# Pooled attention and a tanhshrink FFN on one core: the row of score maxima turned by VectorE instead of TensorE and DRAM

## The chip, the cores and the metric

The kernel runs on one core of a Trainium2 chip. The metric is device time in microseconds (us) of one execution, as the median of several runs. The engines are TensorE (PE for matmuls, PEld for its weight loads), VectorE (DVE), ScalarE (ACT), GpSimd (POOL) and SyncE (SP), which here issues the DMAs.

## The reference

```python
def _attn_ref(q, k, v):                     # q, k, v: (8, 8, 1152, 64) float32
    B, H, S, D = q.shape
    q_pool = q.reshape(B, H, S // 2, 2, D).mean(axis=3)
    scores = (1.0 / np.sqrt(D)) * np.matmul(q_pool, k.transpose(0, 1, 3, 2))
    scores = scores - np.max(scores, axis=-1, keepdims=True)
    attn = np.exp(scores)
    attn = attn / (np.sum(attn, axis=-1, keepdims=True) + 1e-09)
    return np.matmul(attn, v)

def _moe_ref(x, w_in, w_out):               # x (4608, 512), w_in (512, 2048), w_out (2048, 512)
    h = x @ w_in
    g = h - np.tanh(h)
    return g @ w_out
...
    x = attn_out.transpose(0, 2, 1, 3).reshape(B * S, H * D)
    return _moe_ref(x=x, **moe_kwargs)
```

## The kernel before

The work is two stages in a row on one core: attention for 64 heads, then the FFN over 4608 tokens. All products run in the 32-bit format fp32r, and each operand is split into a high part and a rest (`hi`, `lo`), so that a product is the sum of three matmuls. Blocks of FFN weights are split in the same way during the attention, through a PSUM buffer (`w_block`).

Attention takes two heads at a time, a pair, 32 pairs in all. Heads lie on partitions 0 to 63 and 64 to 127. A pair has 36 units (`U`); the first 18 are the scores, the exponentials and the product with v for the first 288 queries, the other 18 the same for the other 288. At every second unit `scores` makes one group: four products of two heads each (`hi·hi`, `hi·lo`, `lo·hi` and `ones_k·mb`, 128 keys by 288 queries) into one PSUM buffer `ps`, and ACT takes the exponential of it into `p_f`. The fourth product subtracts the row of maxima: `mb` holds, on a partition of each head, minus the maximum of each query's scores, and `ones_k` has ones there. At a half's end `pv` multiplies the `p_f` with v, and behind the second half `z_sums` adds up the denominators.

The maxima are made beforehand, one or two pairs ahead. `max_part` multiplies 128 queries with 384 keys in one `hi` part, and DVE reduces the result from PSUM into `mx`; 15 such chunks make a pair. Eight of them run between the groups of the second half, seven between those of the first. `max_rows` then reduces `mx` to `nm`, 128 queries by 10 columns, and turns it into rows: PE transposes it with an identity at the start of the next half (`turn`), ACT copies the high part (`hi`), DVE takes the rest (`lo`), one DMA writes both to DRAM (`m_dram`), and four DMAs bring them back as two rows for each head of `mb`.

```python
        units = dict(load=-80, query_sums=-62, hi=-55, lo=-36, load_v=-30)
        row, steps = -19, (5, 11)
        ...
        if pi == 0:
            row, steps = -43, (3, 4)
```

These numbers are units before a pair's first group; `row` says when `max_rows` runs, `steps` how many units later the store and the loads of the row are put on SP's queue. Each engine runs its instructions in the order in which the units issue them (`InOrder`); all of it passes through the helper's line 37, so the profile gives that line and the names of tiles tell the instructions apart. SP's queue is in order as well: a DMA that waits holds back all behind it, and each waits for the DMA eight places ahead of it in the queue, whose semaphore it shares.

`ps` is a pool of four buffers of two PSUM banks each, for the groups, the chunks, p·v, the transposes and the weight blocks. A request is given the buffer whose last reader stands earliest in the program's order.

Of the kernel before, what the change touches and what calls it, by code (L numbers as in the profile page):

```python
# [8 lines left out]
F32 = mybir.dt.float32  # L9
F32R = mybir.dt.float32r  # L10
I32 = mybir.dt.int32
AF = mybir.ActivationFunctionType
ALU = mybir.AluOpType
AX = mybir.AxisListType
# [29 lines left out]
def kernel(  # L44
# [17 lines left out]
    nc = tc.nc  # L62
    P = 128
    B, NP, _, _, SQ = q.shape
# [10 lines left out]
    dram = ctx.enter_context(tc.tile_pool(name="scratch", bufs=1, space=DRAM))  # L75

    ident = const.tile([P, P], F32, name="ident")
# [9 lines left out]
    x_dram = dram.tile([NP, P, NTOK], F32, name="x_dram")  # L87
    z_dram = dram.tile([B, NP, 2, SQ], F32, name="z_dram")
    r_dram = dram.tile([B, NP, 2, SQ], F32, name="r_dram")
    m_dram = dram.tile([2, 10, 2, P], F32, name="m_dram")  # L90
    wi_dram = dram.tile([NF, P, 2, NP, P], F32, name="wi_dram")
    wo_dram = dram.tile([NF, P, 2, DM], F32, name="wo_dram")

# [41 lines left out]
    t, n = chunks.pop()  # L135
# [4 lines left out]
    with ExitStack() as actx:  # L140

        sm = actx.enter_context(tc.tile_pool(name="sm", bufs=2))
        op = actx.enter_context(tc.tile_pool(name="op", bufs=1))
# [7 lines left out]
        pe, act, dve, pool, sp = (InOrder(tc, e) for e in (nc.tensor, nc.scalar, nc.vector, nc.gpsimd, nc.sync))  # L151

        HQ = SQ // 2
        CH = S // 3
# [5 lines left out]


        mb = [op.tile([P, SQ], F32R, name=f"mb{i}") for i in range(2)]
        ones_k = op.tile([P, P], F32R, name="ones_k")
        for x in (*mb, ones_k):
            nc.gpsimd.memset(x.bitcast(F32), 0.0)
        for h in range(2):
            nc.gpsimd.memset(ones_k[64 * h:64 * h + 2].bitcast(F32), 1.0)


        at, first, early = {}, {}, {}  # L170

        def banks(dtype=F32):
            return ps_a.tile([P, 2, 512], dtype, name="ps")
# [3 lines left out]
        def add(u, f, *args, at=at):  # L177
            at.setdefault(u, []).append(lambda: f(*args))
# [22 lines left out]
        def query_sums(pi, eng):  # L201

            w = pairs[pi]
            eng.tensor_tensor(w.kq[:, 0:SQ], w.q_n[:, 0], w.q_n[:, 1], op=ALU.add)
            w.mx = sm.tile([P, 5, 2, 3], F32, name="mx")
            w.hi = hl.tile([P, KQ], F32R, name="hi")
            w.lo = hl.tile([P, KQ], F32R, name="lo")

# [8 lines left out]
        def max_part(u, pi, t, c):  # L217


            w = pairs[pi]  # L220
            ps = banks()
            q0 = min(t * P, SQ - P)
            mv = slice(SQ + c * CH, SQ + (c + 1) * CH)
            for h in range(2):
                r = slice(64 * h, 64 * h + 64)
                pe.matmul(ps[:, h, 0:CH], w.hi[r, q0:q0 + P], w.hi[r, mv], start=True, stop=True)
            add(u + 1, lambda: dve.tensor_reduce(w.mx[:, t, :, c], ps[:, :, 0:CH], axis=AX.X, op=ALU.max), at=first)

        def max_rows(u, pi, steps):

            w = pairs[pi]
            nm = sm.tile([P, 10], F32, name="nm")
            dve.tensor_reduce(nm, w.mx.rearrange("p t h c -> p (t h) c"), axis=AX.X, op=ALU.max, negate=True)
            mt = sm.tile([10, 2, P], F32R, name="mt")
            md = m_dram[w.i]

            def turn():
                w.ps_t = banks()[0:10, 0, 0:P]
                pe.transpose(w.ps_t, nm, ident)

            def hi():
                act.activation(mt[:, 0], w.ps_t, AF.Copy)

            def lo():
                dve.tensor_tensor(mt[:, 1], w.ps_t, mt[:, 0].bitcast(F32), op=ALU.subtract)

            def there():
                sp.dma_start(md, mt.bitcast(F32))

            def back():  # L250
                by_head = md.rearrange("(t h) s n -> h s t n", h=2)
                for h in range(2):
                    rows = w.mb[64 * h:64 * h + 2].bitcast(F32)
                    sp.dma_start(rows[:, 0:4 * P].rearrange("s (t n) -> s t n", n=P), by_head[h, :, 0:4])
                    sp.dma_start(rows[:, 4 * P:], by_head[h, :, 4, 5 * P - SQ:])
            add(u + 1, turn, at=first)
            add(u + 2, hi, at=first)
            add(u + 3, lo, at=first)
            add(u + steps[0], there)
            add(u + steps[1], back)  # L260

        def scores(w, half, kt, p):

# [138 lines left out]
        for i, blk in enumerate(blocks):  # L402
            u = U * (i - 2) + 5 if i else 23
# [17 lines left out]
        for i, t in enumerate((wi, wi, wi, wo, wi, wo)):  # L421
            f = len(t)
# [4 lines left out]
        for pi in range(n_pair):  # L427
            u = pi * U
            units = dict(load=-80, query_sums=-62, hi=-55, lo=-36, load_v=-30)
            row, steps = -19, (5, 11)  # L430

            spots = [x for half, us in ((-54, (2, 4, 8, 10, 12, 14, 16)), (-36, (2, 4, 8, 10, 14, 16)))
                     for x in [(early, half)] + [(at, half + i) for i in us]]
            if pi == 0:
                units.update(load=-70, query_sums=-62, hi=-60, lo=-41, load_v=-40)
                spots = [(at, -60 + i) for i in range(15)]
                row, steps = -43, (3, 4)
            if pi == 1:
                units.update(load=-104)
            add(u + units["load"], load, pi)  # L440
            add(u + units["query_sums"], query_sums, pi, dve if pi < 1 else pool)
            for c in range(0, KQ, SQ):
                add(u + units["hi"], hi_part, pi, c, c + SQ)
            add(u + units["lo"], lo_part, pi)
            for i, (when, x) in enumerate(spots):
                add(u + x, max_part, u + x, pi, i // 3, i % 3, at=when)
            add(u + units["load_v"], load_v, pi)
            add(u + row, max_rows, u + row, pi, steps)

        def run(u, at=at):  # L450

# [8 lines left out]
        for u in range(end + 60):  # L460
            run(u, first)
            run(u, early)
            n, r = divmod(u, G)
# [21 lines left out]
    pe, pool, sp = (InOrder(tc, e) for e in (nc.tensor, nc.gpsimd, nc.sync))  # L485
# [81 lines left out]
    for ci, (t0, n) in enumerate(chunks):  # L567
        x_h, x_l, _ = xs
        po = []
        for fc in range(NF):  # L570
# [11 lines left out]
            g = hidden(x_h, x_l, n, fc)  # L582
# [44 lines left out]
```

## Time and profile before

| what | value |
|---|---|
| median of 3 runs | 1634.48 us (1634.25 to 1634.59) |
| profiled execution | 1634.2 us, span 1632.4 us |
| busy share of the span | PE 99%, PEld 76%, DVE 75%, ACT 63%, POOL 53% |
| DMA queue of SP | 72512 packets, 145.80 MB, 27.3% of 16 engines |
| attention | from the start to about 835 us |
| FFN | from there to the end |

A row of the timeline gives start and length in us, engine, line, operation, output and inputs, shape, how many in a row, and in brackets how long the engine sat idle before it and what ended that. A row of a group gives busy time in us, mean length in ns, and idle time ahead of it. "issue" as a releaser means that the profile shows nothing that the engine waited for. Matmuls overlap, so the length of one is not the time until the next; that is read from the starts.

### The profile page before, as it was taken

The numbers are of one execution on the slowest core, as the hardware profiler recorded it, in microseconds if no ns is written. First come the engines' busy times: TensorE is split into PE (matmuls) and PEld (weight loads), VectorE is DVE, ScalarE is ACT, GpSimd is POOL, SyncE is SP. The second block draws the span as 40 slices with busy tenths as digits, with TensorE's granted clock in tenths as the row PEclk, the third lists the DMA queues.
The fourth block names the chain that finished last, engine by engine and source line by source line (L and its number), as shares of the span: only waits on it lengthen the run. The fifth ranks groups of instructions, "written<-read, shape, count | busy, mean of one in ns | idle before, by whom it ended". The sixth has DMA issues, their size and how long they took to land.

```text
span 1632.4 us, 32106 instructions
## 1 busy us (share of the span) xinstructions
PE 1611.2 (99%) x12576; PEld 1246.3 (76%) x12576; DVE 1226.8 (75%) x1725; ACT 1023.4 (63%) x1865; POOL 873.3 (53%) x694
## 2 busy tenths in 40 slices
PE   6999999999999999999999999999999999999999
PEld 3777777777777777777778888888888888888898
DVE  7877778787777777777648776777777777777786
ACT  2656665666556656665566666666665766666786
POOL 2776767667667676676754243434343342423332
PEclk9999999999999999999999999999999999999999
DMA  3343443443434434344546111101010111000000
GB/s 142 121 139 117 140 134 108 127 130 133 127 108 142 134 114 126 123 140 146 157 177 229 39 39 35 31 26 53 26 53 26 39 40 39 27 33 20 33 21 27
DMA packets 72664, 147.86 MB, mean 91 GB/s; under 512 B 11136, under 2 KB 36672, under 8 KB 72512
## 3 DMA queue, kind: packets, MB, share of 16 engines
q1 hardware_dynamic: 72512, 145.80, 27.3%
q8 instruction: 99, 1.62, 0.4%
q14 instruction: 53, 0.43, 0.1%
HBM read 109.49 MB, written 36.27 MB: 89 GB/s over the span
## 4 chain that ended last, share of the span: by engine, by line
PE 97%; DVE 2%; ACT 0%; DMA 0%; issue 0%; ACTq 0%
PE ps L37 49%; PE ps_h L37 24%; PE ps_o L37 24%; DVE mx L37 1%; DMA q_n<-in_q_dram 0%; ACT hi L37 0%; ACT p_f L37 0%; DVE lo L37 0%; DVE kq L37 0%; DVE w L37 0%; DVE ps L37 0%; ACT x L562 0%; ACT z_s L37 0%; ACT mt L37 0%; DVE nm L37 0%
## 5 line engine op out<-in xcount | busy, mean ns | idle before, releaser
L37 DVE TENSOR_REDUCE mx<-ps 128x2 f32<-128x768 f32 x480 | 434.8, 951 | 139.0 <-PE ps L37 138.9
L37 POOL TENSOR_TENSOR g_lo<-g_s,g_hi 128x512 fp32r<-128x512 f32 (+1 forms) x160 | 190.7, 1192 | 483.1 <-ACT g_hi L530 445.0
L37 ACT ACTIVATE p_f<-ps 128x576 f32<-128x576 f32 x576 | 362.7, 650 | 83.5 <-PE ps L37 67.4
L37 POOL TENSOR_TENSOR z<-p_f 128x576 f32<-128x576 f32 x192 | 275.2, 1433 | 236.7 <-ACT p_f L37 236.7
L37 PE MATMUL ps<-hi 64*128 64x288 f32 (+1 forms) x2112 | 318.0, 355 | 13.4 <-ACT hi L37 8.3
L37 PE MATMUL ps_h<-x,wi 128*128 128x512 f32 (+1 forms) x1440 | 318.3, 370 | 0.0
L37 PE MATMUL ps_o<-wo,g_hi 128*128 128x512 f32 x1008 | 311.7, 391 | 0.0
L37 PE MATMUL ps<-p_f,v 128*64 128x288 f32 x2304 | 293.5, 409 | 0.1
L37 PEld LDWEIGHTS ps_h<-x,wi 128*128 128x128 f32 x1440 | 253.3, 188 | 50.3
L37 PEld LDWEIGHTS ps<-hi 64*128 64x128 f32 x2112 | 195.8, 188 | 79.8 <-DVE mx L37 22.9
L37 PEld LDWEIGHTS ps<-p_f,v 128*64 128x64 f32 x2304 | 159.8, 137 | 113.7 <-ACT p_f L37 12.2
L519 ACT ACTIVATE g_u<-ps_h 128x512 f32<-128x512 f32 (+1 forms) x160 | 88.8, 555 | 236.3 <-PE ps_h L37 236.3
L524 DVE SCALAR_TENSOR_TENSOR ps_w<-g_u,ps_h 128x512 f32<-128x512 f32 (+1 forms) x160 | 103.2, 645 | 157.6 <-ACT g_t L520 157.0
L37 PEld LDWEIGHTS ps_o<-wo,g_hi 128*128 128x128 f32 x1008 | 187.7, 188 | 39.0
L37 PE MATMUL ps_o<-wo,g_lo 128*128 128x512 f32 x504 | 196.4, 390 | 0.0
L37 POOL TENSOR_TENSOR z<-z,p_f 128x576 f32<-128x576 f32 x128 | 183.1, 1431 | 10.0
L37 ACT ACTIVATE o_s<-ps 128x288 f32<-128x288 f32 x64 | 26.3, 411 | 231.8 <-PE ps L37 231.8
L37 PE MATMUL ps<-lo,hi 64*128 64x288 f32 x1152 | 171.2, 294 | 0.0
L37 PE MATMUL ps<-hi,lo 64*128 64x288 f32 x1152 | 171.1, 293 | 0.0
L37 PE MATMUL ps<-mb,ones_k 64*128 64x288 f32 x1152 | 170.6, 292 | 0.0
L529 DVE COPY_PREDICATED g_s<-g_m,g_t 128x512 f32<-128x512 int32 (+1 forms) x160 | 115.1, 719 | 16.7 <-DVE g_s L528 0.5
L527 DVE SCALAR_TENSOR_TENSOR ps_w<-g_s,ps_w 128x512 f32<-128x512 f32 (+1 forms) x160 | 102.9, 643 | 16.6 <-ACT g_m L523 0.5
(70 smaller groups left out, 2248.3 us busy)
## 6 DMA issues: line engine op xcount, KB each, us to landing
q_n<-in_q_dram SPq DMA_DIRECT2D x32, 576.0 KB
kq<-in_k_dram SPq DMA_DIRECT2D x32, 576.0 KB
v<-in_v_dram SPq DMA_DIRECT2D x32, 576.0 KB
x_dram<-o_s SPq DMA_DIRECT2D x32, 288.0 KB
out_dram<-o_s SPq DMA_DIRECT2D x34, 256.0 KB
w_raw<-in_moe_w_in_dram SPq DMA_DIRECT2D x16, 512.0 KB
wi_dram<-w_hl SPq DMA_DIRECT2D x16, 512.0 KB
w_raw<-in_moe_w_out_dram SPq DMA_DIRECT2D x16, 512.0 KB
```

Of the source, the lines that this page charges most:

```text
L37: ins = self.tc.keep_in_program_order(f(*args, **kwargs))
L519: nc.scalar.activation(u, h, AF.Square)
L524: nc.vector.scalar_tensor_tensor(w, u, -P0, h, op0=ALU.add, op1=ALU.mult)
L527: nc.vector.scalar_tensor_tensor(w, s2, P2, w, op0=ALU.add, op1=ALU.mult)
L529: last = nc.vector.copy_predicated(s1, m.bitcast(I32), th).ins
```

## The change

The turn of the maxima leaves PE, ACT and DRAM. `nm` becomes a fixed tile of 128 x 32 whose columns 10 to 31 stay zero; DVE transposes it in blocks of 32 by 32 right behind the reduction, so that in `tr` the row of column c lies on partitions c, c + 32, c + 64 and c + 96, 32 queries on each. Ten DMAs, one for each head and group of 128 queries, put these pieces straight into one row of `mb` for each head. The row goes in one part instead of a high part and a rest, so `ones_k` has one row of ones for each head. The order inside `mx` is heads first. The DMAs stand at `row` + 3, and for pair 0 at `row` + 1.

```diff
-    m_dram = dram.tile([2, 10, 2, P], F32, name="m_dram")
...
+        nms = [op.tile([P, 32], F32R, name=f"nm{i}") for i in range(2)]
...
-        for x in (*mb, ones_k):
+        for x in (*nms, *mb, ones_k):
...
-            nc.gpsimd.memset(ones_k[64 * h:64 * h + 2].bitcast(F32), 1.0)
+            nc.gpsimd.memset(ones_k[64 * h:64 * h + 1].bitcast(F32), 1.0)
...
-            w.mx = sm.tile([P, 5, 2, 3], F32, name="mx")
+            w.mx = sm.tile([P, 2, 5, 3], F32, name="mx")
...
-        def max_rows(u, pi, steps):
+        def max_rows(u, pi, step):
...
-            nm = sm.tile([P, 10], F32, name="nm")
-            dve.tensor_reduce(nm, w.mx.rearrange("p t h c -> p (t h) c"), axis=AX.X, op=ALU.max, negate=True)
-            mt = sm.tile([10, 2, P], F32R, name="mt")
-            md = m_dram[w.i]
-            def turn():
-                w.ps_t = banks()[0:10, 0, 0:P]
-                pe.transpose(w.ps_t, nm, ident)
-            def hi():
-                act.activation(mt[:, 0], w.ps_t, AF.Copy)
-            def lo():
-                dve.tensor_tensor(mt[:, 1], w.ps_t, mt[:, 0].bitcast(F32), op=ALU.subtract)
-            def there():
-                sp.dma_start(md, mt.bitcast(F32))
+            nm, tr = nms[w.i], sm.tile([P, 32], F32, name="tr")
+            dve.tensor_reduce(nm[:, 0:10], w.mx.rearrange("p h t c -> p (h t) c"), axis=AX.X, op=ALU.max, negate=True)
+            dve.transpose(tr, nm.bitcast(F32))
             def back():
-                by_head = md.rearrange("(t h) s n -> h s t n", h=2)
-                for h in range(2):
-                    rows = w.mb[64 * h:64 * h + 2].bitcast(F32)
-                    sp.dma_start(rows[:, 0:4 * P].rearrange("s (t n) -> s t n", n=P), by_head[h, :, 0:4])
-                    sp.dma_start(rows[:, 4 * P:], by_head[h, :, 4, 5 * P - SQ:])
-            add(u + 1, turn, at=first)
-            add(u + 2, hi, at=first)
-            add(u + 3, lo, at=first)
-            add(u + steps[0], there)
-            add(u + steps[1], back)
+                for t in range(5):
+                    for h in range(2):
+                        row, c = w.mb[64 * h:64 * h + 1].bitcast(F32), 5 * h + t
+                        if t < 4:
+                            sp.dma_start(row[:, t * P:(t + 1) * P].rearrange("p (g n) -> p g n", n=32), tr[c:P:32])
+                        else:
+                            sp.dma_start(row[:, t * P:].rearrange("p (g n) -> p g n", n=32), tr[P - (SQ - t * P) + c:P:32])
+            add(u + step, back)
...
-            row, steps = -19, (5, 11)
+            row, step = -19, 3
...
-                row, steps = -43, (3, 4)
+                row, step = -43, 1
```

The instructions move at three places. On PE, from the end of the first half's p·v (`p_f,v`) into the second half, before (`ident,nm` is the transpose; a chunk of maxima is `hi` with 128x384; a group of scores is the four products with 128x288):

```order
L37 MATMUL ps<-hi 128x384 x2
L37 MATMUL ps<-p_f,v 64x288 x18
L37 MATMUL ps<-ident,nm 10x128
L37 MATMUL ps<-hi 128x384 x2
L37 MATMUL ps<-hi 128x288 x2
L37 MATMUL ps<-lo,hi 128x288 x2
L37 MATMUL ps<-hi,lo 128x288 x2
L37 MATMUL ps<-mb_117,ones_k 128x288 x2
L37 MATMUL ps<-hi 128x288 x2
```

After:

```order
L37 MATMUL ps<-hi 128x384 x2
L37 MATMUL ps<-p_f,v 64x288 x18
L37 MATMUL ps<-hi 128x384 x2
L37 MATMUL ps<-hi 128x288 x2
L37 MATMUL ps<-lo,hi 128x288 x2
L37 MATMUL ps<-hi,lo 128x288 x2
L37 MATMUL ps<-mb_116,ones_k 128x288 x2
L37 MATMUL ps<-hi 128x288 x2
```

The transpose is gone; everything else on PE keeps its order. The buffers of `ps` are dealt out anew: before, the second chunk of the half (`hi` 128x384 behind two groups) takes the buffer of the first chunk, the third group that of the first, the third chunk that of the transpose, the fourth group that of the second. After, the second chunk takes the buffer of p·v, the third group that of the first chunk, the third chunk that of the first group, and the fourth group, as before, that of the second.

On DVE, from the reduction to `nm` in the first half's p·v through the eight chunks of the second half, before (`w_...` and `ps` with 128x512 are the block of weights):

```order
L37 TENSOR_REDUCE mx<-ps 128x2 x7
L37 TENSOR_REDUCE nm<-mx 128x10
L37 TENSOR_SCALAR ps<-w_1410 128x512
L37 SCALAR_TENSOR_TENSOR w_1591<-w_raw,ps 128x512
L37 TENSOR_REDUCE mx<-ps 128x2
L37 TENSOR_TENSOR mt<-ps,mt 10x128
L37 TENSOR_REDUCE mx<-ps 128x2 x7
L37 TENSOR_SCALAR ps<-ps 128x512
L37 TENSOR_SCALAR w_1788<-ps 128x512
```

After:

```order
L37 TENSOR_REDUCE mx<-ps 128x2 x7
L37 TENSOR_REDUCE nm_117<-mx 128x10
L37 STREAM_TRANSPOSE tr<-nm_117 128x32
L37 TENSOR_SCALAR ps<-w_1417 128x512
L37 SCALAR_TENSOR_TENSOR w_1598<-w_raw,ps 128x512
L37 TENSOR_REDUCE mx<-ps 128x2 x8
L37 TENSOR_SCALAR ps<-ps 128x512
L37 TENSOR_SCALAR w_1796<-ps 128x512
```

The transpose stands right behind `nm`, and the subtraction `mt`, which stood between the first and the second chunk, is gone.

On SP's queue, from one load of weights to the next, before:

```order
L37 DMA w_raw<-in_moe_w_out_dram 128x1024
L37 DMA v<-in_v_dram 128x1152
L37 DMA wi_dram<-w_hl 256x4x128
L37 DMA m_dram<-mt 10x256
L37 DMA wi_dram<-w_hl 256x4x128
L37 DMA q_n<-in_q_dram 128x1152
L37 DMA kq<-in_k_dram 128x1152
L37 DMA mb_117<-m_dram 2x4x128
L37 DMA mb_117<-m_dram 2x64
L37 DMA mb_117<-m_dram 2x4x128
```

After:

```order
L37 DMA w_raw<-in_moe_w_out_dram 128x1024
L37 DMA v<-in_v_dram 128x1152
L37 DMA wi_dram<-w_hl 256x4x128
L37 DMA mb_116<-tr 1x4x32 x8
L37 DMA mb_116<-tr 1x2x32 x2
L37 DMA wi_dram<-w_hl 256x4x128
L37 DMA q_n<-in_q_dram 128x1152
```

Ten small loads of `mb` stand ahead of `q_n` and `kq`, where four stood behind them, and the store to `m_dram` is gone.

More of the change, by code (lines that the diff above doesn't have):

```diff
@@ L226, in max_part @@
                 pe.matmul(ps[:, h, 0:CH], w.hi[r, q0:q0 + P], w.hi[r, mv], start=True, stop=True)
-            add(u + 1, lambda: dve.tensor_reduce(w.mx[:, t, :, c], ps[:, :, 0:CH], axis=AX.X, op=ALU.max), at=first)
-        def max_rows(u, pi, steps):
+            add(u + 1, lambda: dve.tensor_reduce(w.mx[:, :, t, c], ps[:, :, 0:CH], axis=AX.X, op=ALU.max), at=first)
+        def max_rows(u, pi, step):
             w = pairs[pi]
-            nm = sm.tile([P, 10], F32, name="nm")
-            dve.tensor_reduce(nm, w.mx.rearrange("p t h c -> p (t h) c"), axis=AX.X, op=ALU.max, negate=True)
-            mt = sm.tile([10, 2, P], F32R, name="mt")
-            md = m_dram[w.i]
-            def turn():
-                w.ps_t = banks()[0:10, 0, 0:P]
-                pe.transpose(w.ps_t, nm, ident)
-            def hi():
-                act.activation(mt[:, 0], w.ps_t, AF.Copy)
-            def lo():
-                dve.tensor_tensor(mt[:, 1], w.ps_t, mt[:, 0].bitcast(F32), op=ALU.subtract)
-            def there():
-                sp.dma_start(md, mt.bitcast(F32))
-            def back():
-                by_head = md.rearrange("(t h) s n -> h s t n", h=2)
-                for h in range(2):
-                    rows = w.mb[64 * h:64 * h + 2].bitcast(F32)
-                    sp.dma_start(rows[:, 0:4 * P].rearrange("s (t n) -> s t n", n=P), by_head[h, :, 0:4])
-                    sp.dma_start(rows[:, 4 * P:], by_head[h, :, 4, 5 * P - SQ:])
-            add(u + 1, turn, at=first)
-            add(u + 2, hi, at=first)
-            add(u + 3, lo, at=first)
-            add(u + steps[0], there)
-            add(u + steps[1], back)
@@ L447 @@
             add(u + units["load_v"], load_v, pi)
-            add(u + row, max_rows, u + row, pi, steps)
+            add(u + row, max_rows, u + row, pi, step)
         def run(u, at=at):
```

## The prediction

> **What bounds the kernel now.** I read the page's busy shares and its chain first, then the waits, then the timeline of one pair and of the start.
>
> ```profile
> span 1632.4 us, 32106 instructions
> PE 97%; DVE 2%; ACT 0%; DMA 0%; issue 0%; ACTq 0%
> ```
>
> TensorE (PE) sets the end: 97% of the chain is its own work. Only two things move the time: what PE issues, and what PE waits for. "Busy" counts overlapping matmuls, so I read PE from start to start. The change touches the attention half alone; everything after 835 us is issued as before and I cost it at nothing.
>
> The place that matters is the second half of a pair's scores, from the transpose that follows the first half's p·v product to the next p·v. I call it the slot; mxN and ktN are its chunk of maxima and its group of scores, in the order that PE issues them (mx18, kt0, kt1, mx20, kt2, mx22, kt3, kt4, mx26 and so on; the number of an mx is its unit). Timeline of pair 15's slot, PE and PE's weight loads first, then VectorE (DVE), then ScalarE (ACT):
>
> ```profile
> 419.12 4.59 PE L37 MATMUL ps<-p_f,v 128*64 128x288 f32 x36
> 423.64 0.28 PE L37 MATMUL ps<-ident,nm 128*10 128x128 f32 x1
> 423.84 0.58 PE L37 MATMUL ps<-hi 64*128 64x384 f32 x4
> 424.26 0.30 PE L37 MATMUL ps<-lo,hi 64*128 64x288 f32 x2
> 424.66 0.30 PE L37 MATMUL ps<-hi 64*128 64x288 f32 x2
> 425.34 0.50 PEld L37 LDWEIGHTS ps<-hi 64*128 64x128 f32 x4 [0.23 <-DVE mx L37]
> 425.89 0.30 PE L37 MATMUL ps<-lo,hi 64*128 64x288 f32 x2
> 431.11 4.59 PE L37 MATMUL ps<-p_f,v 128*64 128x288 f32 x36
> ...
> 420.35 0.18 DVE L37 TENSOR_REDUCE nm<-mx 128x10 f32<-128x30 f32 x1
> 424.33 0.96 DVE L37 TENSOR_REDUCE mx<-ps 128x2 f32<-128x768 f32 x1 [2.42 <-PE ps L37]
> 425.78 0.28 DVE L37 TENSOR_TENSOR mt<-ps,mt 10x128 fp32r<-10x128 f32 x1 [0.49 <-ACT mt L37]
> 425.99 1.80 DVE L37 TENSOR_REDUCE mx<-ps 128x2 f32<-128x768 f32 x2
> 428.00 4.42 DVE L37 TENSOR_REDUCE mx<-ps 128x2 f32<-128x768 f32 x5 [0.21 <-PE ps L37]
> ...
> 423.75 0.41 ACT L37 ACTIVATE o_s<-ps 128x288 f32<-128x288 f32 x1 [2.27 <-PE ps L37]
> 424.95 0.65 ACT L37 ACTIVATE p_f<-ps 128x576 f32<-128x576 f32 x1 [0.78 <-PE ps L37]
> 425.50 0.25 ACT L37 ACTIVATE mt<-ps 10x128 fp32r<-10x128 f32 x1
> 425.65 0.62 ACT L37 ACTIVATE p_f<-ps 128x576 f32<-128x576 f32 x1
> ```
>
> The transpose occupies PE from 423.64 to 423.84. Then its PSUM buffer, one of four, stays taken until DVE's mt ends at 426.06, so mx20 must reuse mx18's buffer and waits until DVE ends mx18 at 425.29, and kt2 waits for the exponential of kt0.
>
> The last pairs show the slot without chunks of maxima, with the transpose (pair 30) and without (pair 31):
>
> ```profile
> 801.54 0.28 PE L37 MATMUL ps<-ident,nm 128*10 128x128 f32 x1
> 806.77 4.59 PE L37 MATMUL ps<-p_f,v 128*64 128x288 f32 x36
> 818.50 4.59 PE L37 MATMUL ps<-p_f,v 128*64 128x288 f32 x36
> 823.01 0.40 PE L37 MATMUL ps<-hi 64*128 64x288 f32 x2
> 828.00 1.19 PE L37 MATMUL ps<-p_f,v 128*64 128x288 f32 x8
> ```
>
> With it the slot takes 806.77 − 801.54 = 5.23 us, without 828.00 − 823.01 = 4.99: 0.24 less. The p·v before it takes the same either way (423.64 − 419.12 = 4.52; 823.01 − 818.50 = 4.51), so no drain goes with the transpose.
>
> **The change, part by part.**
>
> *Transpose off PE.* Worth 0.20 us (423.64 to 423.84) in each of 31 slots, if nothing else waits; the 32nd lies in the start.
>
> ```profile
> L37 PE MATMUL ps<-ident,nm 128*10 128x128 f32 x32 | 8.9, 278 | 3.1 <-DVE nm L37 3.1
> ```
>
> *Buffer, ACT copy and DVE subtract gone.* I follow the slot by hand with durations of its rows: scores 0.53 (kt0 starts 424.13, 0.13 ahead of the row at 424.26; kt1 at 424.66); a chunk 0.17; from a chunk's start to its reduction 0.49 (423.84 to 424.33); a reduction 0.96 alone, 0.90 in a run; from a score's start to its exponential 0.82 (424.13 to 424.95), then 0.65, 0.62 in a run; from a buffer's release to PE's next product up to 0.16 (425.60 to 425.76). Run on the old buffers this gives back the observed start of p·v within 0.1. With the new ones: mx18 at 423.64, kt0 423.93, kt1 424.46; mx20 takes the buffer of the p·v, free since ACT's copy ended at 424.16, and starts at 424.99 (was 425.34); kt2 takes mx18's, free at 425.09, and starts at 425.15 (was 425.76, 0.13 ahead of the row at 425.89). Then the next limit shows: kt3 needs kt1's buffer, whose exponential ends at 425.99, so about 426.1; mx26 goes at 427.16; kt5 waits for DVE's mx22 and goes at 427.47. From there DVE's 0.90 a chunk against PE's 0.70 for a chunk and a group, and ACT's exponentials, pace the slot as before. mx34 goes at 430.46, and p·v, 0.27 behind it, at 430.73 instead of 431.11. So 0.38 us a slot, the transpose's 0.20 in it: what is late next is the reductions. Thirty slots (pairs 0 to 29) have chunks: 30 × 0.38 = 11.4. Pair 30's gives 0.2. Bounds: 0.20 if the reductions take all else back; 1.12 if every wait goes too, since the slot takes 431.11 − 423.64 = 7.47 and would then take 4.99 + 8 × 0.17 = 6.35. I take the followed value; it lies nearer to 0.20 because the run of five reductions stays.
>
> *VectorE's transpose added, 128x32.* Not in this trace. Its nearest rows are the memset of the same shape, 0.09, and the reduction nm, 0.18; the farthest that could be like it is mt, 0.28. I take 0.15. It follows nm at 420.35, and DVE idles 2.42 us ahead of mx18, which hides it; without that cover it would cost its length per slot.
>
> ```profile
> 0.91 0.09 DVE L84 MEMSET ones<- 128x32 f32 x1
> ```
>
> *DMAs.* Five small ones a pair become ten, on SP's queue, ahead of q_n and kq and behind the weights' store. The row's trip through DRAM goes.
>
> ```profile
> 22.92 0.36 SPq L37 DMA_DIRECT2D m_dram<-mt  x1
> 24.32 1.15 SPq L37 DMA_DIRECT2D mb<-m_dram  x4
> ...
> 427.42 1.17 SPq L37 DMA_DIRECT2D mb<-m_dram  x4
> 438.38 0.29 PE L37 MATMUL ps<-mb,ones_k 64*128 64x288 f32 x2
> ```
>
> Four issue in 1.17, so ten in 2.9. They can leave at 420.7, when SP has issued all that stands before them; the first reader is at 438.38, 17.7 us later. The first small store was issued at 22.92 and its reader left at 24.32, so one lands within 1.4 us; even ten landing one after another need 14. Cost nothing. q_n and kq, next in the queue, no longer wait for m_dram to be filled behind the slot's first reductions, and leave no later than now: nothing. If this cover went, PE would stand for the lateness once a pair.
>
> *ones_k over one row, memsets of nm, the order inside mx:* same sizes on PE and DVE, POOL idle at the start: nothing.
>
> *The start.* Here DVE bounds, and nm's followers lie on the path:
>
> ```profile
> 20.75 1.95 DVE L37 TENSOR_TENSOR lo<-kq,hi 128x1728 fp32r<-128x1728 f32 x1
> 23.59 7.01 DVE L37 TENSOR_REDUCE mx<-ps 128x2 f32<-128x768 f32 x8 [0.70 <-PE ps L37]
> 25.51 0.36 SPq L37 DMA_DIRECT2D w_raw<-in_moe_w_in_dram  x1
> 29.62 0.63 ACT L37 ACTIVATE ps<-w_raw 128x512 f32<-128x512 f32 x1 [6.24 <-DMA w_raw<-in_moe_w_in_dram]
> 35.45 0.61 PE L37 MATMUL ps<-hi 64*128 64x288 f32 x2 [0.77 <-DVE mx L37]
> 38.57 0.41 PE L37 MATMUL ps<-mb,ones_k 64*128 64x288 f32 x2
> 39.40 0.29 PE L37 MATMUL ps<-mb,ones_k 64*128 64x288 f32 x2
> ```
>
> Without the transpose and the copy, ACT and PE prepare pair 1 early, and the eight reductions can follow lo. lo now ends at 22.70 (20.75 + 1.95); behind the added 0.15 and nm's full length it ends near 22.95, so the eight start 0.6 earlier than 23.59. Against it, v of pair 0 now queues between the ten small DMAs and the first w_raw: that leaves near 24.8 instead of 25.51, with v's bytes ahead, and ACT waits for it ahead of the first exponentials. Products come at half pace until about 38.6 (0.24 from row to row, 0.13 after), once PE has run unbroken since 35.45, that is 3.1 us. A break there would cost up to half of 3.1, 1.6; the gain is at most the 0.9 between 22.70 and 23.59. I take 0.4 gained, nearer to the 0.6 than to the loss because the reductions, not w_raw, set the pace up to 30.6 (23.59 + 7.01). The Trainium skill (TensorE: Matmul & The Clock Gate, Part 1) says that the array runs at half clock until a window of about 3.4 us has been busy; the trace's 3.1 agrees, and by that rule alone the start would gain 0.6.
>
> Sum: 11.4 + 0.2 + 0.4 = 12.0. The profiled execution took 1634.2 (span 1632.4 and 1.8 around it), so 1622.2; the median of the runs shown is 0.3 higher, 1634.5, so **1622.5 us**.
>
> **The rivals.**
>
> - *Only the transpose's own 0.20 is won,* because DVE's five reductions in a row (428.00, 4.42 us) absorb the rest: 31 × 0.2 = 6.2, 1628.3. For it: the run of five ends after p·v has begun (432.42). Against it: DVE waited 0.21 before that run and 0.49 before mt, so the run itself can start earlier.
> - *All waits of the slot go:* 30 × 1.12 = 33.6, 1600.9. Against it: DVE's 0.90 against PE's 0.70.
> - *Slower: the ten transfers land one after another and the row is late.* From 1.77 us each (17.7 / 10) they outlast the cover; at 2.2 us PE would stand 4.3 a pair, less the 0.38: 30 × 3.9, about 1752. Against it: 1.4 us for a round trip. The Trainium skill (DMA: Bandwidth & Descriptors, Anatomy of one DMA — SWDGE (gpsimd) path) gives a fixed cost of about 2.0 us a DMA, for another issuing path than SP's; by that figure ten in a row would be late by 2.3 a pair and the estimate would be about 1692, but the trace shows 1.4.
> - *VectorE's transpose is long.* Hidden up to 2.4; at 2.8 it eats the 0.38, and the time stays: about 1634. No row speaks for it; the longest like it is 0.28.
>
> **How the numbers follow.** Forecast (0.3 to 0.5 a slot) 0.68; only the 0.20, 0.16; all waits gone 0.06; transfers late 0.04; long transpose or a start that eats the gain 0.06. What a measurement here can tell from no change is 0.2%, 3.3 us. The first three are faster, 0.90; the last is the same, 0.06; late transfers are slower, 0.04. The range takes in the 0.20 case and 0.7 us of loss in the start, 1629, and on the other side 0.55 a slot with 0.9 in the start, 1617; the ends of 1.12 a slot and of late transfers stay out, 0.16 with the long transpose.
>
> **What would show it.** From p·v to p·v across the slot 11.60 instead of 431.11 − 419.12 = 11.99; the other half unchanged; no ident rows; a transpose of 0.1 to 0.3 right behind nm; PE's wait for DVE's mx at mx20 gone, one for ACT's p_f at kt3 instead; the ten small DMAs issued by 424 and no PE wait on a DMA. Wrong would be: a slot that shrinks by 0.2 or by far more, PE waiting at the mb products, or a start later than before.

## The result and the profile after

The changed kernel takes 1623.88 us (median of 6 runs, 1623.18 to 1624.11) against 1634.57 for the kernel before beside it (6 runs, 1634.25 to 1635.22): a ratio of 0.9933, 95% interval 0.992 to 0.9946. The forecast was 1622.5. That it came within 1.4 us is partly luck: two of its terms were wrong, in opposite directions.

The profiled execution of the kernel after takes 1624.07 us (span 1622.3). By its page PE is busy for 1598.7 us, 99% of the span as before, so the reading goes from p·v to p·v again. The timeline of the kernel after, pair 15's slot: PE and a weight load of PE, then DVE and SP's queue; after the line of dots, two later starts of p·v on PE.

```profile
416.35 4.59 PE L37 MATMUL ps<-p_f,v 128*64 128x288 f32 x36
420.87 0.57 PE L37 MATMUL ps<-hi 64*128 64x384 f32 x4
422.22 0.55 PE L37 MATMUL ps<-hi 64*128 64x384 f32 x4
423.46 0.30 PE L37 MATMUL ps<-lo,hi 64*128 64x288 f32 x2
424.40 0.48 PE L37 MATMUL ps<-hi 64*128 64x384 f32 x4
427.89 0.95 PE L37 MATMUL ps<-p_f,v 128*64 128x288 f32 x6
425.37 0.19 PEld L37 LDWEIGHTS ps<-hi 64*128 64x128 f32 x2 [0.20 <-ACT p_f L37]
417.93 0.21 DVE L37 STREAM_TRANSPOSE tr<-nm 128x32 f32<-128x32 f32 x1 [0.19 <-DMA v<-in_v_dram]
421.35 0.96 DVE L37 TENSOR_REDUCE mx<-ps 128x2 f32<-128x768 f32 x1 [1.84 <-PE ps L37]
424.77 4.42 DVE L37 TENSOR_REDUCE mx<-ps 128x2 f32<-128x768 f32 x5 [0.35 <-PE ps L37]
418.17 5.33 SPq L37 DMA_DIRECT2D mb<-tr  x10
...
787.24 4.59 PE L37 MATMUL ps<-p_f,v 128*64 128x288 f32 x36
817.88 4.59 PE L37 MATMUL ps<-p_f,v 128*64 128x288 f32 x36
```

The slot takes 427.89 − 416.35 = 11.54 us, where it took 11.99. The median over the thirty slots with chunks is 11.53, and the other half stays at 13.20. No `ident` row is left, and the second chunk of maxima starts at 422.22, 1.35 behind the first (before: 425.34 − 423.84 = 1.50, and the first itself 0.20 later for the transpose). The transpose on DVE takes 0.21, and 1.84 of the idle time that covered it is left. The ten DMAs are issued by 423.50 (418.17 + 5.33), and the first product that reads their rows starts at 435.16.

The start of the kernel after, timeline of SP, DVE, ACT and PE in order of time:

```profile
21.30 5.48 SPq L37 DMA_DIRECT2D mb<-tr  x10
22.97 7.01 DVE L37 TENSOR_REDUCE mx<-ps 128x2 f32<-128x768 f32 x8
27.26 0.43 SPq L37 DMA_DIRECT2D w_raw<-in_moe_w_in_dram  x1
32.50 0.62 ACT L37 ACTIVATE ps<-w_raw 128x512 f32<-128x512 f32 x1 [21.55 <-DMA w_raw<-in_moe_w_in_dram]
35.36 0.93 PE L37 MATMUL ps<-hi 64*128 64x384 f32 x4 [3.91 <-DVE w L37]
38.45 0.61 PE L37 MATMUL ps<-hi 64*128 64x288 f32 x2 [1.13 <-DVE mx L37]
44.62 0.30 PE L37 MATMUL ps<-lo,hi 64*128 64x288 f32 x2
45.28 0.95 PE L37 MATMUL ps<-p_f,v 128*64 128x288 f32 x6
```

And two rows of the kernel before that the prediction had not read: its first p·v on the timeline, and SP's issues of `z_dram` (the three numbers are least, median and greatest ns of one).

```profile
41.12 4.59 PE L37 MATMUL ps<-p_f,v 128*64 128x288 f32 x36
...
L37 SPq DMA_DIRECT2D z_dram<-z_s x32: 500/512/608, 60.7 to 835.9; - x32
```

From start to start of p·v the whole difference is accounted for:

| stretch | before | after | difference | forecast |
|---|---|---|---|---|
| start to the first p·v | 41.12 | 45.28 | +4.16 | −0.4 |
| from there to pair 30's first p·v (797.02; 787.24) | 755.90 | 741.96 | −13.94 | −11.4 |
| from there to the last p·v (828.00; 817.88) | 30.98 | 30.64 | −0.34 | −0.2 |
| from there to the end of the span | 804.4 | 804.4 | 0 | 0 |
| sum | 1632.4 | 1622.3 | −10.1 | −12.0 |

So the slots gave more than forecast, and the start lost 4.16 where a small gain was forecast. The ten small DMAs hold SP for 5.48 us, not 2.9; `w_raw`, behind them and v, leaves at 27.26 instead of 25.51; ACT waits for it until 32.50 (before 29.62), and PE stands 3.91 ahead of 35.36.

Two things make up the 4.16. PE's last break before its full pace ends at 38.45 instead of 35.45, which is 3.00. From there to the first p·v it takes 6.83 instead of 5.67, which is the other 1.16: products go at half pace for 6.17 (to 44.62) instead of 3.4 (35.45 to 38.8). How much of this second part belongs to the change is open, since the full pace also comes at different times behind the same work (last section).

### The profile page after: what moved, and what is told of

Read it like the earlier page. It is cut to its first block, busy times and chain, and to the rows that moved or that the text cites. A ratio compares the mean times of both kernels' runs of the same rounds, so it can differ in the third digit from the quotient of the medians.

```text
span 1622.3 us, 32306 instructions
## 1 busy us (share of the span) xinstructions
PE 1598.7 (99%) x12544; PEld 1242.3 (77%) x12544; DVE 1230.9 (76%) x1725; ACT 1017.4 (63%) x1833; POOL 872.7 (54%) x696
## 5 line engine op out<-in xcount | busy, mean ns | idle before, releaser
L37 ACT ACTIVATE p_f<-ps 128x576 f32<-128x576 f32 x576 | 358.0, 652 | 77.1 <-PE ps L37 59.3
```

Of the source, the lines that this page charges most:

```text
L37: ins = self.tc.keep_in_program_order(f(*args, **kwargs))
```

## The experiments

Each is the kernel after with the edit shown, unless a base is named. A number for a slot is the median of the thirty, or pair 15's where its rows are shown. Runs without an interval are single ones; their evidence is the profile.

### What the start lost

**The ten DMAs behind the first loads.** They move eleven units later for pair 0.

```diff
-                row, step = -43, 1
+                row, step = -43, 12
```

> Changed kernel, with pair 0's ten small DMAs put behind the loads of v and of the first weight block on SP's queue (they wait for VectorE's transpose, the loads wait for nothing). Theory: the changed kernel's first p·v comes at 45.28 us instead of 41.12 because its first w_raw leaves at 27.26 instead of 25.51 and lands at 32.50; with the load early, ScalarE's copy of it no longer waits, the first p·v comes at 40 to 41 us and the time is 1619.0 to 1620.0. Rival: the start is late because PE's pace stays at half for longer whatever the loads do; then the first p·v stays at 44 to 46 and the time at 1623.9. The slots stay at 11.53 either way.

Measured: 1619.82 us (4 runs, 1619.33 to 1621.07), ratio to the kernel before 0.991, interval 0.9894 to 0.9927. Timeline of its start:

```profile
27.43 0.62 ACT L37 ACTIVATE ps<-w_raw 128x512 f32<-128x512 f32 x1 [16.46 <-DVE mx L37]
32.10 0.93 PE L37 MATMUL ps<-hi 64*128 64x384 f32 x4 [0.63 <-DVE w L37]
34.84 0.61 PE L37 MATMUL ps<-hi 64*128 64x288 f32 x2 [0.77 <-DVE mx L37]
39.72 0.30 PE L37 MATMUL ps<-lo,hi 64*128 64x288 f32 x2
41.09 4.59 PE L37 MATMUL ps<-p_f,v 128*64 128x288 f32 x36
```

ACT no longer waits for `w_raw`, PE's stand falls from 3.91 to 0.63, and the first p·v comes at 41.09, as before the change. The slot stays 11.53. So the place of the ten DMAs ahead of the first loads made the loss, and all runs of this version lie below all of both kernels.

**Only v ahead.** The load of v goes ahead of the ten DMAs, and these stay ahead of `w_raw`.

```diff
-                units.update(load=-70, query_sums=-62, hi=-60, lo=-41, load_v=-40)
+                units.update(load=-70, query_sums=-62, hi=-60, lo=-41, load_v=-44)
```

> Changed kernel, with only v of pair 0 put ahead of the ten small DMAs; w_raw stays behind them. If the bytes of v ahead of w_raw are most of the loss, w_raw lands 4.1 us after its issue as in the kernel before, near 30.9, and the first p·v comes near 43; if the issue time of the ten DMAs is most of it, w_raw leaves at 26.8 and ScalarE's copy of it still waits until 31 or later, and the first p·v comes at 43.5 to 45.

Measured: 1621.89 us. Timeline of its start:

```profile
36.99 0.61 PE L37 MATMUL ps<-hi 64*128 64x288 f32 x2 [1.11 <-DVE mx L37]
43.08 3.13 PE L37 MATMUL ps<-p_f,v 128*64 128x288 f32 x24
```

PE stands 2.54 for the weights. The first p·v comes at 43.08, between 41.09 and 45.28: 2.20 before the one and 1.99 behind the other. These differences contain the half pace, which lasts 4.5 here (to 41.5), 4.9 in the version above (to 39.7) and 6.17 in the kernel after. PE's last break, up to which products go at half pace in all three, divides the loss without it: 38.45 − 36.99 = 1.46 hangs on v's place and 36.99 − 34.84 = 2.15 on the ten issues themselves; both have a share. The remaining 0.58 of the 4.19 is the half pace. Each of the three is one profile.

### What the slot won

Five runs put parts of the old turn back. Their rows are shown together behind them.

**The transpose on PE put back, dead** (its result is not used).

```diff
+            def dead():
+                pe.transpose(banks()[0:10, 0, 0:P], nm[:, 0:10].bitcast(F32), ident)
+            add(u + 1, dead, at=first)
```

> Changed kernel, plus the old transpose on PE into a buffer that nobody reads. Theory (the transpose's own time lies on PE's path): p·v to p·v across the slot 11.73 instead of 11.53, that is 0.20 more. Rival (the reductions pace the slot, and PE's time before them is absorbed): 11.53 to 11.60.

Measured: 1629.79 us, slot 11.74, which is 0.20 to 0.21 more. Pair 30's slot, which has no chunks, goes from 9.51 to 9.72. The transpose is worth its time on PE, no more.

**The whole old turn put back, dead:** PE's transpose, ACT's copy and DVE's subtraction; the store to DRAM and the loads stay away.

```diff
+            mt = sm.tile([10, 2, P], F32R, name="mt")
+            def turn():
+                w.ps_t = banks()[0:10, 0, 0:P]
+                pe.transpose(w.ps_t, nm[:, 0:10].bitcast(F32), ident)
+            def hi():
+                act.activation(mt[:, 0], w.ps_t, AF.Copy)
+            def lo():
+                dve.tensor_tensor(mt[:, 1], w.ps_t, mt[:, 0].bitcast(F32), op=ALU.subtract)
+            add(u + 1, turn, at=first)
+            add(u + 2, hi, at=first)
+            add(u + 3, lo, at=first)
```

> Changed kernel, plus the whole old turn on PE, ScalarE and VectorE (transpose, copy, subtraction) into a tile that nobody reads; the rows still go by the new way. Theory (all of the slot's gain is the engines' work and the buffer it holds, none of it the trip through DRAM): slot 11.95 to 12.00. Rival (some of the gain comes from the DMAs): 11.75 to 11.90.

Measured: 1638.52 us, slot 11.99, the same as before the change. All of the slot's gain is thus the three instructions and their buffer, and none the trip through DRAM. (The time is above that of the kernel before mostly because the start stays late, with the first p·v at 44.06; besides, three of its slots take 12.26, 12.27 and 13.24, and why is open.)

**Only the buffer held,** taken where the transpose was and given back where the subtraction was, by copies of one column on DVE.

```diff
+            kept = sm.tile([P, 1], F32, name="kept")
+            def take():
+                w.ps_t = banks()[:, 0, 0:1]
+                dve.tensor_copy(w.ps_t, nm[:, 0:1].bitcast(F32))
+            def give():
+                dve.tensor_copy(kept, w.ps_t)
+            add(u + 1, take, at=first)
+            add(u + 3, give, at=first)
```

> Changed kernel, plus a PSUM buffer taken at the place of the old transpose and given back at the place of the old subtraction, by two copies of one column on VectorE; no work on PE or ScalarE. Theory (the gain beside the transpose's 0.20 is the buffer): slot 11.53 plus 0.15 to 0.25, 11.68 to 11.78. Rival (it is the work of ScalarE and VectorE between the reductions): 11.53 to 11.60.

Measured: 1628.51 us, slot 11.65, so +0.12: short of the 0.15 to 0.25 of the theory and above the rival's 0.07. Buffers were not dealt as they had been before the change either (the third group took the held buffer), so this bounds the buffer's share rather than measures it. It also shows that the sentence on the buffer dealt, in the section on the kernel before, is only roughly true.

**Copy and subtraction alone,** from SBUF: no transpose, no buffer.

```diff
+            mt = sm.tile([10, 2, P], F32R, name="mt")
+            def hi():
+                act.activation(mt[:, 0], w.kq[0:10, 0:P], AF.Copy)
+            def lo():
+                dve.tensor_tensor(mt[:, 1], w.kq[0:10, 0:P], mt[:, 0].bitcast(F32), op=ALU.subtract)
+            add(u + 2, hi, at=first)
+            add(u + 3, lo, at=first)
```

> Changed kernel, plus ScalarE's copy and VectorE's subtraction of 10 x 128 at the places of the old ones, reading a tile in SBUF; no transpose and no PSUM buffer. The transpose alone gave 0.20 of the slot's 0.46 and the buffer alone 0.12. If the parts add up, this gives the remaining 0.14: slot 11.64 to 11.70. Rival (the copy and the subtraction fit into idle time, and the rest is the buffer being held until the subtraction's late end): 11.53 to 11.58.

Measured: 1632.68 us, slot 11.83, so +0.30, more than either side expected. Timeline of DVE in pair 15's slot:

```profile
426.39 0.28 DVE L37 TENSOR_TENSOR mt<-kq,mt 10x128 fp32r<-10x128 f32 x1 [0.53 <-ACT mt L37]
```

DVE stands 0.53 for ACT's copy, and the second reduction, behind the subtraction, starts 6.70 behind p·v (426.60 − 419.90), where the kernel after has 6.25. PE's fifth group waits for that reduction (0.09 us).

**The copy alone.** The same without the subtraction.

```diff
+            mt = sm.tile([10, P], F32R, name="mt")
+            def hi():
+                act.activation(mt, w.kq[0:10, 0:P], AF.Copy)
+            add(u + 2, hi, at=first)
```

> The kernel after, with ACT's copy of 10x128 alone at its old place in the second half (from kq in SBUF, its result unused); VectorE's subtraction, the transpose on PE and the PSUM buffer stay away. With copy and subtraction together the slot took 11.83 instead of 11.53. Theory A: VectorE's stand of 0.53 for ACT's copy and the 0.28 of the subtraction, ahead of the second reduction, made the 0.30. Then the copy alone costs nothing that VectorE sees: slot 11.53 to 11.59, first half unchanged at 13.20, time 1624 to 1626. Theory B: the copy's 0.2 to 0.25 on ACT, ahead of the second exponential, holds the release of that group's buffer and so the fourth group: slot 11.70 to 11.83, time 1629 to 1632.7. In between (11.60 to 11.69) both have a share.

Measured: 1628.82 us, slot 11.70, so +0.17: theory B, at the low end of its bounds. In each timeline of pair 15's slot the reader is to see the first half's p·v, the run of five reductions, and the next p·v.

Timeline with the transpose put back (PE, DVE, PE):

```profile
418.65 4.59 PE L37 MATMUL ps<-p_f,v 128*64 128x288 f32 x36
427.28 4.42 DVE L37 TENSOR_REDUCE mx<-ps 128x2 f32<-128x768 f32 x5 [0.35 <-PE ps L37]
430.39 0.95 PE L37 MATMUL ps<-p_f,v 128*64 128x288 f32 x6
```

Timeline with the whole turn put back:

```profile
422.26 4.59 PE L37 MATMUL ps<-p_f,v 128*64 128x288 f32 x36
431.12 4.42 DVE L37 TENSOR_REDUCE mx<-ps 128x2 f32<-128x768 f32 x5 [0.20 <-PE ps L37]
434.24 0.95 PE L37 MATMUL ps<-p_f,v 128*64 128x288 f32 x6
```

Timeline with the buffer held:

```profile
417.48 4.59 PE L37 MATMUL ps<-p_f,v 128*64 128x288 f32 x36
426.02 4.42 DVE L37 TENSOR_REDUCE mx<-ps 128x2 f32<-128x768 f32 x5 [0.21 <-PE ps L37]
429.14 1.19 PE L37 MATMUL ps<-p_f,v 128*64 128x288 f32 x8
```

Timeline with the copy and subtraction:

```profile
419.90 4.59 PE L37 MATMUL ps<-p_f,v 128*64 128x288 f32 x36
428.62 4.42 DVE L37 TENSOR_REDUCE mx<-ps 128x2 f32<-128x768 f32 x5 [0.22 <-PE ps L37]
431.74 0.95 PE L37 MATMUL ps<-p_f,v 128*64 128x288 f32 x6
```

Timeline with the copy alone, where the second row is ACT's copy and the third the second product of the fourth group:

```profile
417.92 4.59 PE L37 MATMUL ps<-p_f,v 128*64 128x288 f32 x36
424.08 0.29 ACT L37 ACTIVATE mt<-kq 10x128 fp32r<-10x128 f32 x1
425.19 0.30 PE L37 MATMUL ps<-lo,hi 64*128 64x288 f32 x2
426.50 4.42 DVE L37 TENSOR_REDUCE mx<-ps 128x2 f32<-128x768 f32 x5 [0.52 <-PE ps L37]
429.62 1.68 PE L37 MATMUL ps<-p_f,v 128*64 128x288 f32 x12
```

| kernel | p·v to run of five | run of five to next p·v | slot |
|---|---|---|---|
| before | 8.88 | 3.11 | 11.99 |
| after | 8.42 | 3.12 | 11.54 |
| transpose | 8.63 | 3.11 | 11.74 |
| whole turn | 8.86 | 3.12 | 11.98 |
| buffer | 8.54 | 3.12 | 11.66 |
| copy and subtraction | 8.72 | 3.12 | 11.84 |
| copy | 8.58 | 3.12 | 11.70 |

From the run's start on, every slot takes the same 3.11 to 3.12, while DVE works through its five reductions without a break. That these set it is not shown: in the kernel after PE's waits inside the run end with ACT's exponentials (0.20 ahead of 425.37), and no run makes the reductions or the exponentials shorter. Either way, all that the turn costs is what it delays the fourth chunk, the one that starts the run. The copy does so through the fourth group: it stands ahead of the second exponential on ACT, and the group that needs the released buffer has its second product 7.27 behind p·v (425.19 − 417.92) instead of 7.11 (423.46 − 416.35). With the subtraction it is 0.30, with the transpose's 0.21 some 0.51, against 0.44 to 0.46 for the whole turn. So the three instructions account for all of it by their sum, and the buffer, 0.12 by itself, need add nothing to them. The parts overlap and cannot be added up exactly; the three without the buffer were not run together.

### Does the cover hold?

**Every small DMA twice,** on the version with the DMAs behind the loads.

```diff
-                for t in range(5):
+                for t in (*range(5), *range(5)):
```

> The kernel with the loads ahead of pair 0's rows, and every one of the ten small DMAs sent twice, twenty a pair. Theory (the cover of 17 us takes them in every pair but the first): SP issues for 10.6 us a pair and slots and other halves stay at 11.53 and 13.19; pair 0 alone is late, since its rows land near 33 instead of 28, so the first p·v comes 3 us later than with ten. Rival (the ten already use up the cover): PE waits ahead of the mb products and each pair grows by up to 5 us.

Measured: 1624.15 us, 4.3 above its base. Timeline: its start, and, after a line left out, its end.

```profile
21.16 10.85 SPq L37 DMA_DIRECT2D mb<-tr  x20
30.49 1.15 PE L37 MATMUL ps<-mb,ones_k 64*128 64x288 f32 x2 [0.38 <-DMA mb<-tr]
...
802.98 1.37 DVE L37 TENSOR_TENSOR kq<-kq 128x512 f32<-128x512 f32 x1 [6.21 <-DMA kq<-r_dram]
```

In the pairs nothing moves (slot 11.53, other half 13.20): twice the DMAs stay hidden, as forecast. At the start the rows are late by only 0.38, and the first p·v comes at 40.53, earlier than in its base (41.09), not 3 us later: the expectation was wrong there. PE has its full pace by 38.1 here, and only by 39.7 in the base. The loss lies at the end of the attention, where DVE waits 6.21 for a load that stands behind the twenty on SP's queue; the stretches from p·v to p·v there grow from 11.63 to 15.34 and from 9.50 to 10.49.

### Why one of these DMAs takes SP 0.5 us

**Four neighbouring partitions** instead of four that lie 32 apart; the rows then hold wrong maxima.

```diff
-   sp.dma_start(row[:, t * P:(t + 1) * P].rearrange("p (g n) -> p g n", n=32), tr[c:P:32])
+   sp.dma_start(row[:, t * P:(t + 1) * P].rearrange("p (g n) -> p g n", n=32), tr[c:c + 4])
...
-   sp.dma_start(row[:, t * P:].rearrange("p (g n) -> p g n", n=32), tr[P - (SQ - t * P) + c:P:32])
+   sp.dma_start(row[:, t * P:].rearrange("p (g n) -> p g n", n=32), tr[c:c + 2])
```

> Changed kernel, with each small DMA reading its four pieces from four neighbouring partitions instead of four that lie 32 apart; the rows then hold the wrong maxima, so the output is not the reference's. If the step of 32 partitions makes the issue long, one issue falls from 0.49 us to 0.25 to 0.35 and the first p·v comes 1.5 us or more earlier than 45.28; if it is the single partition at the other end, or four short pieces, it stays at 0.47 to 0.50 and the start stays.

**One piece from one partition** of another tile; the rows then hold no maxima, and pair 0's need not wait for `tr`.

```diff
-   sp.dma_start(row[:, t * P:(t + 1) * P].rearrange("p (g n) -> p g n", n=32), tr[c:P:32])
+   sp.dma_start(row[:, t * P:(t + 1) * P], w.kq[c:c + 1, 0:P])
...
-   sp.dma_start(row[:, t * P:].rearrange("p (g n) -> p g n", n=32), tr[P - (SQ - t * P) + c:P:32])
+   sp.dma_start(row[:, t * P:], w.kq[c:c + 1, 0:SQ - t * P])
```

> Changed kernel, with each small DMA reading one piece of 512 or 256 bytes from one partition of kq instead of four or two pieces of 128 bytes from tr; the rows then hold no maxima, so the output is not the reference's. If the number of partitions read makes the issue long, it falls from 0.49 us to 0.25 to 0.35 and the first p·v comes earlier than 45.28 by 1.5 us or more; if it is the single partition at the other end, it stays at 0.45 to 0.60.

Measured: 1623.91 and 1619.74 us. Issues of the small DMAs by tile, of the kernel after, of the neighbours, and of the one piece:

```profile
L37 SPq DMA_DIRECT2D mb<-tr x320: 467/492/727, 21.3 to 797.5; - x160
```

```profile
L37 SPq DMA_DIRECT2D mb<-tr x320: 558/573/742, 21.2 to 797.4; - x160
```

```profile
L37 SPq DMA_DIRECT2D mb<-kq x320: 497/587/1672, 5.6 to 793.9; - x160
```

Neither shortens the issue; both lengthen it a little. Stride and number of pieces are excluded as the cause. What makes it 0.49 here and 0.26 for a load of `mb` from DRAM stays open; a single destination partition, which all three share, was not tried apart, and it cannot be all of it, since `z_dram` goes to DRAM and takes 0.51. The 1619.74 comes from pair 0's DMAs leaving early (5.6), with the first p·v at 40.90.

### Two versions that might have been better still

Both on the version with the DMAs behind the loads (1619.82).

**PE kept busy from the beginning:** every chunk of the start is multiplied three times into the same buffer.

```diff
-            for h in range(2):
-                r = slice(64 * h, 64 * h + 64)
-                pe.matmul(ps[:, h, 0:CH], w.hi[r, q0:q0 + P], w.hi[r, mv], start=True, stop=True)
+            for _ in range(3 if u < 0 else 1):
+                for h in range(2):
+                    r = slice(64 * h, 64 * h + 64)
+                    pe.matmul(ps[:, h, 0:CH], w.hi[r, q0:q0 + P], w.hi[r, mv], start=True, stop=True)
```

> The kernel with the loads ahead of pair 0's rows, with every chunk of maxima before the first group of scores multiplied three times over into the same buffer; only the last is used. It does nothing for the data. Theory (what is left of the start's uncertainty is PE's pace, which becomes full only once PE has been busy without a break for 3 to 6 us; chunks at 0.87 us with idle time between them never get there): PE runs at full pace before 20 us, the products after 30 us stand 0.13 apart, the first p·v comes at 37.5 to 39.5 instead of 41.09 and the time is 1616.5 to 1618.5. Rival (the reductions alone bound the start until the first p·v): 41 and 1619.8, or later if the extra products delay the reductions.

Measured: 1622.11 us (5 runs, 1620.58 to 1623.01), ratio 0.992, interval 0.9907 to 0.9934; first p·v at 43.20. The windows of this kernel, whose last three columns are the granted clock, the DMA share and GB/s, and a row of its timeline on PE:

```profile
25.20:28.50 3.30, 3.30 (x24) 2.88 (x20) 3.30 (x5) 0.23 (x1) 0.00 (x0) 0.50 0.01 1
28.60:32.00 3.40, 2.31 (x22) 1.36 (x18) 3.37 (x5) 1.23 (x3) 0.00 (x0) 1.00 0.91 330
32.10:42.20 10.10, 7.57 (x56) 7.14 (x58) 8.06 (x8) 3.53 (x6) 6.74 (x5) 0.50 0.31 115
```

```profile
32.95 0.93 PE L37 MATMUL ps<-hi 64*128 64x384 f32 x4 [1.26 <-DVE w L37]
```

PE did reach full pace before 30 us: the granted clock is 1.00 from 28.6 to 32.0. It was 0.50 in the 3.3 us before that, behind a gap of 2.46 that ended at 24.84, and it is 0.50 again from 32.1 on, inside the gap of 1.26 ahead of 32.95, until 42.2. The Trainium skill (TensorE: Matmul & The Clock Gate, Why this matters for your kernels) asks for no idle gaps over about 3 us between bursts; here the pace went with no gap of PE above 2.46 us between 22 and 45 us. So the first p·v came neither at the theory's 37.5 to 39.5 nor at the rival's 41.

**Two chunks moved** in the second half, so that the first groups wait less for buffers: the second chunk from behind the second group to behind the first, and the third from behind the third to behind the fourth. The run of five reductions becomes one of six.

```diff
-            spots = [x for half, us in ((-54, (2, 4, 8, 10, 12, 14, 16)), (-36, (2, 4, 8, 10, 14, 16)))
+            spots = [x for half, us in ((-54, (0, 6, 8, 10, 12, 14, 16)), (-36, (2, 4, 8, 10, 14, 16)))
```

> The kernel with the loads ahead of pair 0's rows, with the slot's chunks of maxima behind groups 0, 3, 4, 5, 6, 7 and 8 instead of 1, 2, 4, 5, 6, 7 and 8. Followed by hand in the way of the forecast, the first groups then wait less for buffers: 0.1 to 0.25 us less a slot, 11.3 to 11.45 instead of 11.53, 1612.5 to 1617. Rival (VectorE's six reductions in a row at the end of the slot take it back): 11.53 or more, 1619.8 or more.

Measured: 1622.12 us (5 runs, 1621.83 to 1622.87), ratio 0.9923, interval 0.9911 to 0.9936; slot 11.54, other half 13.26. Timeline of pair 15's slot on DVE and, ahead of it, a row of its start on PE:

```profile
39.72 0.44 PE L37 MATMUL ps<-lo,hi 64*128 64x288 f32 x2
421.57 5.28 DVE L37 TENSOR_REDUCE mx<-ps 128x2 f32<-128x768 f32 x6 [0.74 <-PE ps L37]
```

The rival held: six reductions in a row take back what the earlier chunk gives. The next p·v starts at 425.54, 3.97 behind the run's start; that is 0.85 more than 3.12, for a run that is 5.28 − 4.42 = 0.86 longer. This speaks for DVE as what sets the end of the slot, without showing it for the run of five. The time is above the base's 1619.82 because the other half grows by 0.06, some 2 us in thirty, for a reason that stays open, and because the first p·v comes at 41.63 instead of 41.09.

## Why the prediction was right, and where it was not

- **The slot's mechanism was right, its size a little small.** From the first chunk (420.87) on, the second came 1.35 later (forecast 424.99 − 423.64 = 1.35), the fourth 3.53 later (forecast 427.16 − 423.64 = 3.52), and p·v 7.02 later (forecast 7.09). PE's wait for DVE at the second chunk is gone, and one for ACT's exponential stands at the fourth group instead (0.15 ahead of 423.22), as forecast. The step that missed lies behind the fourth chunk: "from a chunk's start to its reduction 0.49" is the row of the first chunk of a half; at the fourth it measures 424.77 − 424.40 = 0.37. So 0.45 a slot instead of 0.38, some 2 us in thirty.
- **The share of the buffer was told wrongly.** The prediction names copy and subtraction beside the buffer, but what it follows for the gain beyond 0.20 is which buffer comes free when. The runs show that ACT's copy (0.17) and DVE's subtraction, which brings it to 0.30, suffice for it with no buffer held. How the gain divides when all three stand together is not shown.
- **"What is late next is the reductions" fits the runs** (3.12 from the run of five to p·v in every kernel, 3.97 with a run of six), but was not separated from ACT's exponentials, which end PE's waits there.
- **The transpose on DVE** measured 0.21, inside 0.09 to 0.28 and hidden, as forecast.
- **"Four issue in 1.17, so ten in 2.9" was wrong,** and with it the start. They take 5.48. The nearest row was not `mb` from DRAM but `z_dram` from four partitions of SBUF, 0.51 each, which the profile before has; ten of these are 5.1. In the pairs it costs nothing (17.0 us of cover, from 418.17 to the first reader at 435.16); at the start SP's queue is on the path.
- **The start: "0.4 gained, nearer to the 0.6 than to the loss" was wrong.** The eight reductions did start at 22.97, as worked out (22.95). But the sentence that "the reductions, not w_raw, set the pace" fails once `w_raw` leaves at 27.26 instead of the 24.8 forecast. It lands 32.50 − 27.26 = 5.24 later, PE stands 3.91, and half pace lasts until 44.62. The loss was 4.16. The bound of 1.6 counted only the half pace behind a break and not the standing itself, which is 3.00 of it. The prediction's 3.1 of half pace in the kernel before is 3.4: the rows stand 0.24 apart up to 38.8, not 38.6.
- The rivals on the slot's size fell: 0.20 is the transpose alone, and not all waits went. No PE wait on a DMA appears in the pairs.

## What to carry to other kernels

Price an issue on a queue by the row nearest in its source and destination, not by the tile's name, and look at each queue's first use separately: what is free under 17 us of cover in every pair cost 4 us ahead of the first loads, and moving it behind them gave these back. Where a stage ends with a run that takes the same time in every version, as the 3.11 to 3.12 here, only what delays the run's start counts: find that one instruction and follow what holds it. And read a start's loss at PE's last break as well as at its end: behind it the way to full pace took 3.4 to 6.2 us here, and differed even behind the same work.

## What the runs showed of the hardware that was not expected

- SP takes 0.49 to 0.59 us (medians) to issue a DMA of 256 or 512 bytes from SBUF into one partition, whatever its stride and number of pieces, against 0.26 for a load of `mb` from DRAM into two partitions.
- PE's way to full pace is no fixed time after its last break at the start: 3.4 us before the change (35.45 to 38.8), 4.9 with the DMAs behind the loads (34.84 to 39.7), 6.17 after the change (38.45 to 44.62). It is not fixed by the work either: the version with two chunks moved issues the same products as its base at the same times, within 0.01 us, from its last break to 39.48, and then stays at half pace until 40.9 where the base has full pace at 39.7 (the rows at 39.72: 0.44 against 0.30). The Trainium skill (TensorE: Matmul & The Clock Gate, Part 1) says that the activity window runs freely, so that the count of slow products varies from run to run; these two runs agree with that.
- In the run with PE kept busy from the beginning, the granted clock changes at 25.2, 28.6, 32.0 and 42.2 us: 3.4, 3.4 and 10.2 apart, that is one, one and three times 3.4.
